# Weight conversion in an attention and two-layer kernel: the shift on ScalarE, the scaling inside VectorE's product, two early halves

## The chip, the core and the metric

The kernel runs on one core of a Trainium2 chip. A core has five engines with queues of their own: TensorE (PE; its weight loads are shown as PEld), VectorE (DVE), ScalarE (ACT), GpSimd (POOL) and SyncE (SP), which here issues all DMAs. Each engine takes its instructions in order; semaphores hold an instruction back until its inputs are there. The metric is the device time of one execution in microseconds (us).

## The reference

Block-causal attention over 4 batches of 8 heads, 576 positions of 64 dimensions each, and two feed-forward layers of 2304 tokens, width 512, inner width 2048, everything in float32:

```python
scores = where(block_i >= block_j, q @ k.T / 8, -1e9)          # blocks of 64 positions
attn   = exp(scores - max); attn /= attn.sum() + 1e-9
x      = (attn @ v) as 2304 x 512
h = x @ w_in;  x = (relu(h) ** 2) @ w_out                      # layer 0
h = x @ w_in2; out = (h * cos(h)) @ w_out2                     # layer 1
```

## The kernel before

**Attention.** Two heads form a pair, 16 pairs in all. For a pair, TensorE makes the scores of 9 blocks of rows (line 374; block 8 goes to the tile `wide`), VectorE takes their maxima (386), ScalarE the exponentials with their sums (391), GpSimd and VectorE the inverse of the sums (416, 422), GpSimd scales the rows `P` (431). TensorE transposes `P` in groups of four blocks (452); ScalarE rounds each group to `PTh` (457), VectorE keeps the rest as `PTl` (460), which also frees the PSUM bank. TensorE multiplies with the values (517), and ScalarE, VectorE and GpSimd put the two heads' results into `xall` (528, 531, 534, 537). GpSimd also scales the keys (357) and splits the values (486, 492).

The order of these steps on every engine is made by `Plan`: each step has an engine, a cost and a rank; the planner keeps a clock for each engine and takes, among the steps that can start earliest, that of the smallest rank. `RANK` holds an offset for each kind of step, to which ten times the pair's number is added. The order that comes out is the order of the program.

**Weights.** A product in float32 is made of three products of rounded halves (high x high, high x low, low x high), so each weight must be split. The weights come as a packed pair of words of 64 bits, `raw`, with a low and a high word. There are 64 pieces ("halves", class `Half`): 2 layers x 16 channels x 2 (`w0` for the hidden product, `w1` for the output product). Converting one half is: shift (line 205, low word right by 9), mask (212) and rebias (218, ScalarE) of the high word's bits, join (223, puts the lower bits of the high word over the low word), fraction (229, ScalarE, the low word as a float scaled by 2^-43), sign (235), power (241, the exponent alone), high (256, ScalarE, or 259 on GpSimd: the rounded high part) and low (265, fraction times power: the rest). Unless an engine is named, VectorE does it.

The first `EARLY` = 4 halves are steps of the attention plan (`add_half`); the key `late` holds them back until the last pair's first scores, and their rank is 1000. Two more are only loaded there. All others are converted by `convert()`, called while the layers run: one call ends an old half and begins a new one, with four `raw` buffers and two `bits` buffers; fraction is put off to the next call of `flush()`.

**Layers.** Each layer goes over blocks of up to 512 tokens (five in each layer), each block over 16 channels `c`. A step (`hidden`, line 629) makes 12 matmuls into one of four banks `h`; ScalarE and VectorE make `g` of it and split it into `gs` (651, 652, 641, 644 in layer 0; 659, 662, 667, 673, 676 in layer 1); three steps later `output` (line 693) uses it in 12 matmuls. `PACE` says how many conversions are called in a step of each block; the first block converts layer 0, the last block of layer 0 and those behind it convert layer 1, each half when its buffer is free. Before each block but the first, `xall` is split into `xs` (315 on ScalarE, 318 on VectorE), into the same buffers as before.

## Time and profile before

| | |
|---|---|
| median of 3 runs | 1008.35 us (1008.33 to 1009.51) |
| profiled execution, its own time | 1007.74 us |
| its span in the trace | 1006.0 us |
| TensorE busy | 980.9 us (98%) |
| VectorE, ScalarE, GpSimd busy | 624.1, 594.2, 168.4 us |
| mean granted clock of TensorE | 0.996 |

The page of a profile lists the busy time of each engine and the costliest lines. Matmuls are pipelined, and their ends are modelled, so a busy TensorE is not one at its peak. What a change is worth is read from the stage that it touches: attention ends at about 192 us; block 0 of layer 0, with the conversion of its weights, goes to about 289 us; the weights of layer 1 are converted between 500 and 750 us.

### The profile page before, as it was taken

What the parts mean: (1) busy time and instruction counts of PE and PEld (TensorE: products, weight loads), DVE (VectorE), ACT (ScalarE), POOL (GpSimd) and SP (SyncE); (2) the same over time, 40 slices, a digit from 0 to 9 for tenths busy, and PEclk for the clock granted to TensorE, in tenths of its full rate; (3) what the DMA queues carried; (4) which work ended last, traced back from release to release, by engine and by line L of the source; (5) the groups of instructions that cost most, each with busy time, mean ns of one, the idle gap of its engine ahead of it and who ended that gap; (6) DMA issues with size and microseconds to landing.
All of it is one profiled execution on the core that took longest, in us unless ns stands there. A gap on an engine that the chain in (4) does not pass through costs nothing.

```text
span 1006.0 us, 13923 instructions
## 1 busy us (share of the span) xinstructions
PE 980.9 (98%) x4895; PEld 824.7 (82%) x4895; DVE 624.1 (62%) x1260; ACT 594.2 (59%) x1226; POOL 168.4 (17%) x290
## 2 busy tenths in 40 slices
PE   9999999889989999999999999999999999999998
PEld 7878887767768889988888888888888888899996
DVE  6888789899951111221168998976646555656554
ACT  7999999688873344443367886644334333434433
POOL 6888888700000000000000000000000000000000
PEclk9999999999999999999999999999999999999999
DMA  6433321244420000000013432000000100100000
GB/s 219 143 107 123 112 97 63 85 167 168 168 84 1 1 1 1 2 1 1 1 63 115 170 135 84 22 1 35 8 1 1 43 1 1 43 1 1 33 1 31
DMA packets 18806, 58.56 MB, mean 58 GB/s; under 512 B 1968, under 2 KB 2096, under 8 KB 18736
## 3 DMA queue, kind: packets, MB, share of 16 engines
q1 hardware_dynamic: 18736, 57.68, 16.5%
q8 instruction: 38, 0.62, 0.2%
q14 instruction: 32, 0.26, 0.1%
HBM read 52.95 MB, written 4.72 MB: 57 GB/s over the span
## 4 chain that ended last, share of the span: by engine, by line
PE 72%; DVE 19%; ACT 5%; issue 3%; POOL 1%; DMA 0%; SPq 0%; DVEq 0%; ACTq 0%
PE acc L693 32%; PE h L629 31%; PE ps L374 3%; DVE w L265 3%; DVE bits L235 3%; DVE raw L223 3%; PE ps L452 2%; PE ps L517 2%; DVE raw L205 2%; DVE raw L241 2%; DVE nmax L386 2%; DVE gs L644 2%; ACT P L391 1%; ACT PTh L457 1%; DVE PTl L460 1%
## 5 line engine op out<-in xcount | busy, mean ns | idle before, releaser
L629 PE MATMUL h<-xs,w 128*128 128x512 f32 (+2 forms) x1920 | 421.7, 368 | 3.5 <-ACT xs L315 3.0
L629 PEld LDWEIGHTS h<-xs,w 128*128 128x128 f32 x1920 | 344.6, 188 | 60.2 <-ACT xs L315 3.4
L693 PE MATMUL acc<-gs,w 128*128 128x512 f32 (+1 forms) x960 | 215.2, 372 | 9.0 <-DVE gs L644 8.9
L693 PE MATMUL acc<-w,gs 128*128 128x512 f32 x864 | 209.8, 391 | 0.3 <-ACT xall L706 0.3
L693 PEld LDWEIGHTS acc<-gs,w 128*128 128x128 f32 x960 | 168.4, 190 | 43.8 <-DVE gs L644 13.5
L644 DVE TENSOR_TENSOR gs<-g,gs 128x512 fp32r<-128x512 f32 (+2 forms) x160 | 101.1, 633 | 143.6 <-ACT gs L641 143.5
L693 PEld LDWEIGHTS acc<-w,gs 128*128 128x128 f32 x864 | 161.6, 188 | 33.0 <-ACT xall L706 0.8
L641 ACT CAST gs<-g 128x512 fp32r<-128x512 f32 (+2 forms) x160 | 92.3, 577 | 152.6 <-DVE g L676 96.0
L662 DVE SCALAR_TENSOR_TENSOR g<-turns,h 128x512 f32<-128x512 int32 (+1 forms) x80 | 50.7, 634 | 122.2 <-ACT turns L659 121.6
L659 ACT ACTIVATE turns<-h 128x512 int32<-128x512 f32 (+1 forms) x80 | 44.2, 552 | 68.1 <-PE h L629 68.0
L651 ACT ACTIVATE g<-h 128x512 f32<-128x512 f32 (+1 forms) x80 | 43.9, 549 | 67.5 <-PE h L629 66.8
L374 PE MATMUL ps<-kB,qB 128*128 128x64 f32 (+7 forms) x256 | 81.7, 416 | 1.5 <-DVE PTl L460 0.8
L431 POOL TENSOR_SCALAR P<-P,rinv 128x64 f32<-128x64 f32 (+2 forms) x144 | 79.8, 573 | 6.6 <-DVE rinv L422 3.1
L673 ACT ACTIVATE g<-g,half_pi 128x512 f32<-128x512 f32 (+1 forms) x80 | 54.6, 682 | 38.1 <-DVE g L667 38.1
L452 PEld LDWEIGHTS ps<-ident,P 128*128 128x128 f32 (+1 forms) x400 | 49.1, 142 | 27.7 <-issue 14.8
L460 DVE TENSOR_TENSOR PTl<-ps,PTh 128x512 fp32r<-128x512 f32 x96 | 65.2, 686 | 6.9 <-ACT PTh L457 5.4
L391 ACT ACTIVATE P<-ps,nmax 128x64 f32<-128x64 f32 (+7 forms) x128 | 65.4, 513 | 6.4 <-DVE nmax L386 4.9
L452 PE MATMUL ps<-ident,P 128*128 128x128 f32 (+1 forms) x400 | 63.4, 280 | 3.5 <-POOL P L431 3.1
L386 DVE TENSOR_REDUCE nmax<-ps 128x1 f32<-128x64 f32 (+7 forms) x128 | 56.4, 444 | 10.2 <-PE ps L374 9.2
L457 ACT CAST PTh<-ps 128x512 fp32r<-128x512 f32 (+1 forms) x112 | 60.1, 551 | 4.3 <-PE ps L452 3.4
L517 PE MATMUL ps<-PTh,vhl 128*128 128x320 f32 (+3 forms) x224 | 59.5, 299 | 1.2 <-DVE PTl L460 0.7
L218 ACT ACTIVATE bits<-bits,new_bias 128x512 int32<-128x512 int32 x64 | 46.5, 726 | 17.6 <-DVE bits L212 17.6
(52 smaller groups left out, 959.8 us busy)
## 6 DMA issues: line engine op xcount, KB each, us to landing
raw<-in_w_dram SPq DMA_DIRECT2D x64, 512.0 KB, 3.6
qB<-in_qd_dram SPq DMA_DIRECT2D x15, 576.0 KB, 4.0
v_raw<-in_vp_dram SPq DMA_DIRECT2D x16, 320.0 KB, 2.9
kB<-in_kT_dram SPq DMA_DIRECT2D x16, 288.0 KB, 2.8
out_dram<-o SPq DMA_DIRECT2D x8, 512.0 KB, 3.1
out_dram<-o SPq DMA_DIRECT2D x2, 256.0 KB, 2.9
qB<-in_qd_dram SPq DMA_DIRECT2D x1, 384.0 KB, 4.4
qB<-in_qd_dram SPq DMA_DIRECT2D x1, 192.0 KB, 2.9
```

Of the source, the lines that this page charges most:

```text
L374: nc.tensor.matmul(bank[:, 0:w] if one else wide[:, x, 0:w], lhsT=qB[r][:, i].rearrange("p e d -> p (e d)"), rhs=kB[r][:, x * w : (x + 1) ...
L386: nc.vector.tensor_reduce(out=nmax[i], in_=held(), axis=AX.X if one else AX.XY, op=ALU.max, negate=True)
L391: nc.scalar.activation(out=mine if one else mine.rearrange("p (x w) -> p x w", x=2), in_=held(), func=AF.Exp, bias=nmax[i], scale=1.0, acc ...
L431: nc.gpsimd.tensor_scalar(out=mine, in0=mine, scalar1=inverse[:, i - i0 : i - i0 + 1], scalar2=1.0, op0=ALU.mult, op1=ALU.mult,)
L452: nc.tensor.transpose(bank[0:keys, n * 128 : (n + 1) * 128], P[r][:, o : o + keys], ident)
L457: nc.scalar.copy(out=PT[0][0:keys, at], in_=plan.held[s][0][0:keys, 0:w])
L460: nc.vector.tensor_tensor(out=PT[1][:, at] if keys == 128 else PT[0][keys:128, at], in0=bank[0:keys, 0:w], in1=PT[0][0:keys, at].bitcast(F32),
L517: nc.tensor.matmul(bank[:, (a - i0) * D : w], lhsT=vhl[:, j, e].rearrange("p x d -> p (x d)"), rhs=pt[x][:, s0 : s0 + i1 - a, e, :], start ...
L629: nc.tensor.matmul(h, lhsT=w[:, a, kk * 128 : (kk + 1) * 128], rhs=xs[kk].parts[:, x], start=(m == 0), stop=(m == 3 * KD - 1),)
L641: nc.scalar.copy(out=gs[:, 0], in_=g)
L644: nc.vector.tensor_tensor(out=gs[:, 1], in0=g, in1=gs[:, 0].bitcast(F32), op=ALU.subtract)
L693: nc.tensor.matmul(dst, lhsT=lhsT, rhs=rhs, start=(c == 0 and m == 0), stop=(c == KF - 1 and m == 2),)
```

## The change

Shift goes from VectorE to ScalarE, as a multiplication by a little under 2^-9 from integer to integer. Fraction is no longer an instruction of its own: its factor 2^-43 is put into low, which becomes a product of two operations on VectorE (integer low word x 2^-43 x power). `flush`, `later`, `fraction` and `high_beside` fall away; in `convert()` the order is now sign, shift, mask, high, power, rebias, low, join. `EARLY` is 2 instead of 4, and the two early halves round their high part on ScalarE. In the plan they have no `late` any more; a new argument `beside` lets a step hold a second engine's clock, and each of VectorE's five steps of an early half is planned as holding GpSimd as well. All ranks change; the early halves' goes from 1000 to 206.6. `PACE` of the last block of layer 0 goes from 1.75 to 2.

```diff
-    "scores": 3.5,
-    "maximum": -3.1,
+    "scores": 5.2,
+    "maximum": -5.2,
...
-    "weights": 1000,
+    "weights": 206.6,
...
+            if beside:
+                t = max(t, clock[beside])
+                clock[beside] = t + cost
...
-    EARLY = 4
+    EARLY = 2
...
         def shift(self):
-            nc.vector.tensor_scalar(
-                out=self.low_word, in0=self.low_word, scalar1=9, scalar2=None,
-                op0=ALU.logical_shift_right,
+            nc.scalar.activation(
+                out=self.low_word.bitcast(U32), in_=self.low_word.bitcast(U32), func=AF.Copy,
+                scale=2.0**-9 * (1.0 - 2.0**-23),
             )
...
-        def fraction(self):
-            nc.scalar.activation(
-                out=self.low_word.bitcast(F32), in_=self.low_word.bitcast(U32), func=AF.Copy,
-                scale=2.0**-43,
-            )
...
         def low(self):
-            nc.vector.tensor_tensor(
-                out=self.room()[:, 1], in0=self.low_word.bitcast(F32),
-                in1=self.high_word.bitcast(F32), op=ALU.mult,
-            )
+            nc.vector.scalar_tensor_tensor(
+                out=self.room()[:, 1], in0=self.low_word.bitcast(U32), scalar=2.0**-43,
+                in1=self.high_word.bitcast(F32), op0=ALU.mult, op1=ALU.mult,
+            )
...
             new.shift()
+            new.mask()
         if old:
+            old.high()
             old.power()
-            old.high()
         if new:
-            new.mask()
             new.rebias()
         if old:
             old.low()
         if new:
             new.join()
-            later.append(new.fraction)
...
-                plan.add("V", 0.34, rank, x.shift, [late], [raw])
-                plan.add("V", 0.34, rank, x.mask, [high, late], [bits])
...
+                both = dict(beside="G")
+                plan.add("A", 0.56, rank, x.shift, writes=[raw])
+                plan.add("V", 0.45, rank, x.mask, [high], [bits], **both)
...
-        PACE = {0: 2, last: 1.75, last + 1: 0.75}
+        PACE = {0: 2, last: 2, last + 1: 0.75}
```

Lines of the changed kernel have other numbers: 216 is mask, 227 join, 233 sign, 239 power, 257 low, 209 shift; 444 is `PTl` (460 before), 436 the transposes (452), 358 the scores (374), 515 the join into `xall` (531), 627 `gs` low (644).

The first place is VectorE in block 0 of layer 0, one conversion between two `gs` low. Before:

```order
L644 TENSOR_TENSOR gs<-g,gs 128x512
L235 SCALAR_TENSOR_TENSOR bits<-raw,bits 128x512
L205 TENSOR_SCALAR raw<-raw 128x512
L241 TENSOR_SCALAR raw<-bits 128x512
L212 TENSOR_SCALAR bits<-raw 128x512
L265 TENSOR_TENSOR w_2320<-raw 128x512
L223 SCALAR_TENSOR_TENSOR raw<-raw 128x512
```

And now:

```order
L627 TENSOR_TENSOR gs<-g,gs 128x512
L233 SCALAR_TENSOR_TENSOR bits<-raw,bits 128x512
L216 TENSOR_SCALAR bits<-raw 128x512
L239 TENSOR_SCALAR raw<-bits 128x512
L257 SCALAR_TENSOR_TENSOR w_2331<-raw 128x512
L227 SCALAR_TENSOR_TENSOR raw<-raw 128x512
```

The shift is gone, and mask, which stood between power and low, now stands ahead of power.

The second place is TensorE where pair 2's transposes (of `P_98`) stand among pair 3's scores (`ps<-kB,qB`). Before:

```order
L452 MATMUL ps_85<-ident,P_98 128x128 x4
L374 MATMUL ps_87<-kB_94,qB_92 128x256
L452 MATMUL ps_84<-ident,P_98 128x128 x4
L374 MATMUL ps_83<-kB_94,qB_92 128x320
L452 MATMUL ps_86<-ident,P_98 128x128 x4
L374 MATMUL ps_88<-kB_94,qB_92 128x384
L452 MATMUL ps_85<-ident,P_98 128x128 x4
L374 MATMUL ps_87<-kB_94,qB_92 128x448
L452 MATMUL ps_84<-ident,P_98 128x128 x4
L374 MATMUL ps_83<-kB_94,qB_92 128x512
```

And now:

```order
L436 MATMUL ps_84<-ident,P_98 128x128 x4
L358 MATMUL ps_87<-kB_94,qB_92 128x192
L358 MATMUL ps_86<-kB_94,qB_92 128x256
L358 MATMUL ps_85<-kB_94,qB_92 128x320
L358 MATMUL ps_83<-kB_94,qB_92 128x384
L358 MATMUL ps_87<-kB_94,qB_92 128x448
L358 MATMUL ps_88<-kB_94,qB_92 128x512
L436 MATMUL ps_84<-ident,P_98 128x128 x4
L436 MATMUL ps_86<-ident,P_98 128x128 x4
L436 MATMUL ps_85<-ident,P_98 128x128 x4
L436 MATMUL ps_83<-ident,P_98 128x128 x4
```

The scores stand together and the transposes behind them; two pairs on the same happens once more, and from there on the two kinds alternate again.

The third place is VectorE at the last pair, whose transposes are lowered there to `PTl`. Before:

```order
L235 SCALAR_TENSOR_TENSOR bits<-raw,bits 128x512
L205 TENSOR_SCALAR raw<-raw 128x512
L241 TENSOR_SCALAR raw<-bits 128x512
L531 TENSOR_TENSOR xall<-ps_85,half_117 64x320
L265 TENSOR_TENSOR w_2104<-raw 128x512
L212 TENSOR_SCALAR bits<-raw 128x512
L223 SCALAR_TENSOR_TENSOR raw<-raw 128x512
L460 TENSOR_TENSOR PTl<-ps_84,PTh 128x512
L460 TENSOR_TENSOR PTl<-ps_86,PTh 128x512
```

And now:

```order
L406 RECIPROCAL rinv_116<-sums_113 128x2
L444 TENSOR_TENSOR PTl<-ps_83,PTh 128x512
L515 TENSOR_TENSOR xall<-ps_85,half_117 64x320
L444 TENSOR_TENSOR PTl<-ps_84,PTh 128x512
L444 TENSOR_TENSOR PTl<-ps_86,PTh 128x512
```

The conversion's instructions are no longer there; those of the two early halves now stand among pairs 1 to 4 (counted from 0).

## Rows read from the trace of the kernel before

**Rows 1.** Busy us and counts of each engine in four stretches, whole core.
```profile
core 0: us, PE busy (x) PEld busy (x) DVE busy (x) ACT busy (x) POOL busy (x), PEclk, DMA share, GB/s
20.00:50.00 30.00, 29.81 (x193) 25.04 (x194) 24.10 (x58) 28.51 (x85) 26.17 (x43) 1.00 0.48 164
...
180.00:192.00 12.00, 8.86 (x57) 8.16 (x56) 9.71 (x20) 8.42 (x18) 10.28 (x11) 0.86 0.24 88
...
220.00:280.00 60.00, 55.65 (x235) 43.11 (x234) 60.00 (x126) 51.07 (x89) 0.00 (x0) 1.00 0.48 167
300.00:350.00 50.00, 50.00 (x223) 41.40 (x222) 7.52 (x11) 17.74 (x29) 0.00 (x0) 1.00 0.00 1
```

**Rows 2.** Waits of TensorE, 190 to 320 us: us, times, longest.
```profile
PE acc L693 <- DVE gs L644: 8.9, 11, 4.1
```

**Rows 3.** Waits of TensorE, 320 us to the end, its only row.
```profile
PE acc L693 <- ACT xall L706: 0.3, 1, 0.3
```

**Rows 4.** Waits of TensorE, 0 to 205 us.
```profile
PE ps L452 <- POOL P L431: 3.1, 3, 1.1
...
PE ps L374 <- DVE PTl L460: 0.8, 1, 0.8
PE ps L517 <- DVE PTl L460: 0.7, 1, 0.7
```

**Rows 5.** Timeline of TensorE: start, us, what [idle before, releaser].
```profile
185.82 3.04 PE L452 MATMUL ps<-ident,P 128*128 128x128 f32 x13 [1.07 <-POOL P L431]
...
192.06 9.18 PE L629 MATMUL h<-xs,w 128*128 128x512 f32 x38
...
289.25 0.50 PE L629 MATMUL h<-xs,w 128*128 128x512 f32 x1 [2.99 <-ACT xs L315]
```

**Rows 6.** Timeline of VectorE in block 0, one step.
```profile
276.46 0.68 DVE L644 TENSOR_TENSOR gs<-g,gs 128x512 fp32r<-128x512 f32 x1
277.06 0.68 DVE L235 SCALAR_TENSOR_TENSOR bits<-raw,bits 128x512 int32<-128x512 int32 x1
277.67 0.42 DVE L205 TENSOR_SCALAR raw<-raw 128x512 int32<-128x512 int32 x1
278.00 0.42 DVE L241 TENSOR_SCALAR raw<-bits 128x512 int32<-128x512 int32 x1
...
278.68 0.68 DVE L265 TENSOR_TENSOR w<-raw 128x512 fp32r<-128x512 f32 x1
279.28 0.68 DVE L223 SCALAR_TENSOR_TENSOR raw<-raw 128x512 int32<-128x512 int32 x1
...
282.70 0.68 DVE L644 TENSOR_TENSOR gs<-g,gs 128x512 fp32r<-128x512 f32 x1
```

**Rows 7.** Timeline of VectorE in layer 1, two neighbours, the second reading the first.
```profile
606.88 0.69 DVE L662 SCALAR_TENSOR_TENSOR g<-turns,g 128x512 f32<-128x512 int32 x1
607.60 0.43 DVE L667 TENSOR_SCALAR g<-g 128x512 int32<-128x512 int32 x1
```

**Rows 8.** Groups of ScalarE, 207 to 286 us: busy us, mean ns, idle before.
```profile
L218 ACT ACTIVATE bits<-bits,new_bias 128x512 int32<-128x512 int32 x26 | 18.8, 725 | 5.8 <-DVE bits L212 5.8
L229 ACT ACTIVATE raw<-raw 128x512 f32<-128x512 uint32 x25 | 17.0, 678 | 5.5 <-DVE raw L223 5.5
```

**Rows 9.** Timeline of VectorE, the fourth early half's low.
```profile
196.03 0.91 DVE L265 TENSOR_TENSOR w<-raw 128x512 fp32r<-128x512 f32 x1
```

**Rows 10.** Timeline of ScalarE: relu of hidden 1 and of hidden 14, `xs`.
```profile
207.54 0.58 ACT L651 ACTIVATE g<-h 128x512 f32<-128x512 f32 x1
...
286.80 0.57 ACT L651 ACTIVATE g<-h 128x512 f32<-128x512 f32 x1
...
288.58 2.18 ACT L315 CAST xs<-xall 128x512 fp32r<-128x512 f32 x4
```

**Rows 11.** Timeline of GpSimd: an ordinary pair's scaling, the last pair's.
```profile
155.72 3.11 POOL L431 TENSOR_SCALAR P<-P,rinv 128x320 f32<-128x320 f32 x5
...
179.25 4.67 POOL L431 TENSOR_SCALAR P<-P,rinv 128x320 f32<-128x320 f32 x4
```

68 lines of the change are left out of this document (28 added, 40 removed).

## The prediction

> **What bounds the kernel now.** I read the table of stretches first [rows 1]. From 300 to 350 us TensorE is busy for 50.00 of 50 us with VectorE at 7.52: there TensorE sets the pace, and 223 matmuls in 50 us are 5.4 us for the 24 of one step (hidden and output of one channel). From 220 to 280 us it is the other way: VectorE 60.00 of 60, ScalarE 51.07, TensorE 55.65. This is block 0 of layer 0, where every weight is converted as it is first used. The list of waits says the same: TensorE waits 8.9 us for `gs` from VectorE, one wait of 4.1 among them [rows 2]. Later, from 320 us to the end, it waits 0.3 us in all [rows 3], so nothing behind 320 us can be gained. The third loss is the end of attention: the last pair's transposes wait 3.1 us for GpSimd's scaled `P`, and two products wait 0.8 and 0.7 us for `PTl` [rows 4]; TensorE's granted clock is 0.86 of full in 180 to 192 us [rows 1], a mix of its two levels (1.2 and 2.4 GHz) after those waits, and 13 transposes take 3.04 us [rows 5]. Early attention (20 to 50 us) is full: TensorE 29.81 of 30 [rows 1].
>
> So there are three marks. T is the start of the first hidden product, 192.06 in this run. X is the start of block 1's first hidden product, 289.25, after a wait of 2.99 us for `xs` [rows 5]. From X to the end of the span are 1006.0 - 289.25 = 716.75 us, which I keep: they are TensorE's.
>
> **The change part by part.**
>
> *One conversion on VectorE.* One step of block 0 runs from `gs` low at 276.46 to the next at 282.70: 6.24 us, two conversions and one `gs` low [rows 6]. From start to start sign takes 0.61, shift 0.33, power and mask 0.34 each, low 0.60, join 0.60, together 2.82; `gs` low takes 0.60. The change removes the shift (0.33). Low becomes a two-operation form with an integer input; the nearest row, line 662 with an integer and a float input, occupies 0.69 us [rows 7], as low does now (0.68, [rows 6]): nothing to pay. But the new order puts power directly ahead of low, which reads what power writes. Where a dependent instruction stands directly behind its source, it begins only after the source's end: 606.88 + 0.69, next start 607.60, an interval of 0.72 where 0.60 is usual [rows 7]. That gives 0.11 back: power then costs 0.45 instead of 0.34. A conversion is 2.82 - 0.33 + 0.11 = 2.60 and a step 5.8 us; with no such stall it would be 5.6. TensorE's step is 5.4, so VectorE stays the bound, by less.
>
> *One conversion on ScalarE.* Fraction leaves, shift comes: the same Copy over the same integer words. The nearest rows are 0.678 (fraction, line 229) and 0.725 (integer output with a bias, line 218) [rows 8]; I take 0.68, being the same function without a bias. ScalarE's sum a step is unchanged; 51.07 of 60 is busy [rows 1], so it covers this. Dearer, it costs 0.05 x 2 a step, which its idle time covers. Followed through one step (rebias waits for mask, sign for rebias, high for sign) its loop comes out some 0.3 us shorter than VectorE's 5.8.
>
> The Trainium skill ("ScalarE: Activation LUTs", Rules for kernel authors) gives multiplications to VectorE, not ScalarE. The rows bear out the price of one instruction (0.42 as shift on VectorE, 0.68 on ScalarE), but not that it decides here, since VectorE is the full one; by that rule alone the 30 shifts would cost 30 x 0.26 = 8 us.
>
> *Two early halves instead of four, and their place.* Before, two of the four are still being finished when T has come: the fourth ends its low at 196.03 + 0.91 [rows 9], T + 4.9, and GpSimd rounds its high part. Only then does VectorE begin on the layers' own conversions. After, the last pair's rows are followed by the layers' conversions at once. From T: ScalarE needs about 1.0 to empty the last heads' banks (an estimate, two copies), shift starts T + 1.0, rebias is done T + 2.3, the first sign starts there, then 2.60 a conversion with one extra wait of 0.3 for rebias behind the first relu; the relu of hidden 1 comes at T + 9.7. Before, it came at 207.54 [rows 10], T + 15.5. The relu of hidden 14 follows 13 steps later: T + 9.7 + 13 x 5.8 = T + 85.1, before 286.80, T + 94.7 [rows 10]. From there to the first `xs` are 1.78 us (288.58) and 0.67 more to X [rows 5, 10]: X = T + 87.5, before T + 97.2. **Block 0 gives 9.7 us**; bounds 7 (ScalarE's loop at 6.0 a step) and 13 (steps of 5.6 and no wait at the first steps). The two halves that are no longer early cost nothing more: block 0 calls two conversions a step in 16 steps, and before, its last step had only one left. The wait for `xs` stays, since ScalarE's queue still runs behind TensorE.
>
> *End of attention.* VectorE no longer converts between the last pairs' steps. GpSimd's four last tiles took 4.67 us beside that, where five such tiles take 3.11 in an ordinary pair [rows 11]; less the largest (about 0.7) that is 2.4, so 2.3 come back, and the two waits on `PTl` (1.5). **4 us**; at least 0.8 (the last pair has nothing to overlap, and only the `PTl` waits go), at most 3.1 + 1.5 and 1.3 for slow transposes, 5.9.
>
> *The early halves' new place.* They are now done in pairs 1 to 4, behind nothing but attention's own steps. Each adds 5 VectorE instructions (2.9 us), 3 on ScalarE (2.0, at some 0.68) and, for GpSimd, the slowing just named. In 20 to 50 us VectorE has 5.9 idle, GpSimd 3.8, ScalarE only 1.5 [rows 1], and 4.0 are added to ScalarE. Also the table of ranks groups TensorE's work there: six scores in a row, then six groups of transposes, twice, where before they alternate. VectorE frees a transpose group's bank at 0.6 us apiece, slower than TensorE fills them, and the first of the six waits for a bank that VectorE frees only behind five maxima: about 1 us at each place. **I charge 2 us**, between 0 (the idle time swallows it) and 4 (2 at each place).
>
> That DVE work slows GpSimd is what the Trainium skill says in "SBUF — State Buffer" (Who interferes with whom): the pair of ports that both share is locked for a whole instruction. The trace agrees, with the 4.67 us against 2.4. By the lock alone the two halves hold GpSimd for up to 2 x 2.9 = 5.8 us, 2.0 above its idle time: the same charge.
>
> *Second refill* (500 to 640 us). The rate in the last block of layer 0 goes from 1.75 to 2 conversions a step: 1.75 x 2.82 + 0.60 = 5.5 becomes 5.8, against TensorE's 5.4. Over 11 such steps VectorE falls 0.4 x 11 = 4.4 us behind; before, its 9 full steps fell 0.8 x 9 behind less two steps of 2.0 gained, about 3. TensorE then waited 0.3 us at most [rows 3], so 1.4 more should still be covered by the output products that stand between. Zero; up to 2.5 if the cover is gone. Loads keep their place: four raw buffers, each requested when low has read it and used three conversions later (7.8 us).
>
> *Sum.* -9.7 - 4.0 + 2.0 = -11.7. T becomes 190.1, X 277.6, the span 994.3. The profiled execution took 1007.74, 1.74 above its span, and the median of the runs is 1008.35, 0.6 above that: 996.7 on the median's scale. I say **996.5**.
>
> **The rivals.**
> *A: TensorE sets the pace of block 0 too.* If the dependent neighbour costs nothing and attention's end loses all 5.9, steps are 5.6 and little is charged early: 13 + 5.9 - 0.5 = 18, 990. For it: VectorE's plain sum. Against it: two measured intervals of 0.72 and the wait for `xs`.
> *B: ScalarE takes VectorE's place.* Shift, high and rebias now stand in one chain with sign and relu. If semaphores add 0.3 a step, the step is 6.1: block 0 gives 5.8, attention's end 2, the early places cost 3: gain 5, 1003. For it: ScalarE's 51 of 60 [rows 1]. Against it: its sum is unchanged.
> *C: slower: the new ranks open a wait in every pair of attention.* All ranks change, not only those of the weights. TensorE has nearly no idle time there now (0.19 in 30 us, [rows 1]), so each wait is lost. From 13.7/15 = 0.9 us a pair on, the gain of 13.7 (9.7 and 4.0) is eaten; at 1.3 a pair the time is 1008.35 - 13.7 + 19.5 = 1014. For it: ScalarE's 28.51 of 30. Against it: behind pair 4 the order of TensorE alternates scores and transposes as before.
> *D: the change doesn't do what it says*: low's two-operation form takes the shift's 0.33 back. Then a step is 6.4; the relu of hidden 14 comes at T + 10.7 + 13 x 6.4 = T + 93.9, block 0 gives 0.8, and in all 2.8 are left: 1005.5. Line 662's 0.69 speaks against it.
>
> **How the numbers follow.** Forecast (992 to 1000) 0.57, A 0.14, B 0.14, D 0.05, C 0.06, and 0.04 for sums that cancel within 2 us. The runs of one kernel tell 0.2% apart, 2 us. Faster 0.90, same 0.04, slower 0.06. The range reaches over A and most of B and leaves out the rest, about 2 in 10: 989.5 to 1003.5.
>
> **What would show it.** A step of block 0, from `gs` low to `gs` low, is 5.8 us (5.6 is A, 6.1 B, 6.4 D), with power to low 0.45 apart. TensorE's waits in block 0 name `w` from VectorE rather than `gs`. Shift on ScalarE takes 0.68. X minus T is 87.5. T is 190: later than 192 means the new place or the new ranks cost more than the end of attention returns, and the waits of TensorE between 20 and 50 us say which. A wait of over 1 us near 600 us would mean that the second refill is no longer covered.

## The result, and the profile after

The changed kernel takes 1000.3 us (median of 4 runs, 998.36 to 1001.27) against 1008.93 us of the kernel before in the same comparison: a ratio of 0.9911, interval 0.9894 to 0.9929. That is 8.6 us less; the forecast was 996.5, by a sum of 11.7 less. The profiled execution took 1001.27 us, the slowest of the four, with a span of 999.4 us against 1006.0, so the traces below differ by 6.6 us. The other 2 us of the gain lie between these two executions and the medians, and no trace places them.

Four marks divide the span. W is the first product into `wide`, the 576-wide scores, of pair 0 (9.45 us before, 9.69 after; the start-up in front of it differs by some tenths from one execution to another). The last pair's wide is the same product of the last pair. T is the first hidden product, X the first hidden product of block 1, as in the prediction.

```
                        before   after   difference   forecast
W                         9.45    9.69      +0.24        -
W to last pair's wide   155.83  159.73      +3.90       +2.0
last pair's wide to T    26.78   21.15      -5.63       -4.0
T to X                   97.19   88.31      -8.88       -9.7
X to end of span        716.75  720.52      +3.77        0
```

The sum is -6.6. The first three terms went the way the prediction says, each with its size somewhat off; the last was not foreseen at all. The lines that answer to [rows 1], busy time by stretch, with three stretches more:

```profile
core 0: us, PE busy (x) PEld busy (x) DVE busy (x) ACT busy (x) POOL busy (x), PEclk, DMA share, GB/s
20.00:50.00 30.00, 28.14 (x181) 23.48 (x182) 26.91 (x61) 28.63 (x81) 24.97 (x41) 1.00 0.49 164
180.00:192.00 12.00, 10.79 (x77) 9.63 (x76) 7.06 (x16) 9.06 (x22) 8.04 (x13) 1.00 0.00 1
...
220.00:280.00 60.00, 57.08 (x235) 42.59 (x234) 58.23 (x112) 54.56 (x95) 0.00 (x0) 0.99 0.55 183
270.00:290.00 20.00, 17.19 (x61) 12.95 (x60) 14.72 (x27) 15.04 (x27) 0.00 (x0) 0.83 0.37 120
550.00:600.00 50.00, 49.39 (x217) 40.33 (x216) 47.04 (x90) 43.84 (x76) 0.00 (x0) 1.00 0.50 167
```

In 20 to 50 us TensorE lost 1.7 us of busy time and 12 products. At the end of attention (180 to 192) it gained 1.9 us and runs at a clock of 1.00 instead of 0.86. In block 0 VectorE is still all but full. In 270 to 290 the clock is 0.83 where it was 1.00 before, and in 550 to 600, where the second refill runs, 217 matmuls stand for 223.

TensorE's waits from 190 to 320 us, after, answer to [rows 2] (us in total, times, longest; the last two lines are of its weight loads):

```profile
PE h L612 <- ACT xs L299: 2.8, 1, 2.8
PE h L612 <- ACT w L254: 1.2, 1, 1.2
PEld h L612 <- DVE w L257: 5.9, 13, 0.6
PEld h L612 <- ACT w L254: 4.1, 13, 1.6
```

The 8.9 us for `gs` are gone. TensorE is now held back at its weight loads: 13 times by the low part of `w` from VectorE and 13 times by the high part from ScalarE, which itself waits for VectorE's sign (shown further down). A hidden group takes 3.10 us from start to start (270.11 to 273.21) instead of 2.72. The transition to block 1 in TensorE's timeline (start, us, what, idle before):

```profile
270.11 3.26 PE L612 MATMUL h<-xs,w 128*128 128x512 f32 x12
273.21 2.88 PE L676 MATMUL acc<-gs,w 128*128 128x512 f32 x12
278.88 5.79 PE L612 MATMUL h<-xs,w 128*128 128x512 f32 x12 [2.79 <-ACT xs L299]
284.46 3.33 PE L676 MATMUL acc<-gs,w 128*128 128x512 f32 x12
287.63 2.88 PE L612 MATMUL h<-xs,w 128*128 128x512 f32 x12
```

X comes after a wait of 2.79 us (before 2.99, [rows 5]). But the 12 products behind it take 5.58 us from start to the next start; before they took 3.39 (289.25 to 292.64, with 0.23 of waiting for the next `xs` in it). That, and 0.45 in the next group (3.17 instead of 2.72), is the fall of the clock: 2.6 us in this execution, which the prediction did not have.

One step of VectorE in block 0, which answers to [rows 6]:

```profile
271.28 0.69 DVE L627 TENSOR_TENSOR gs<-g,gs 128x512 fp32r<-128x512 f32 x1
271.88 0.68 DVE L233 SCALAR_TENSOR_TENSOR bits<-raw,bits 128x512 int32<-128x512 int32 x1
272.48 0.42 DVE L216 TENSOR_SCALAR bits<-raw 128x512 int32<-128x512 int32 x1
272.82 0.42 DVE L239 TENSOR_SCALAR raw<-bits 128x512 int32<-128x512 int32 x1
273.34 0.69 DVE L257 SCALAR_TENSOR_TENSOR w<-raw 128x512 fp32r<-128x512 uint32 x1
...
277.16 0.68 DVE L627 TENSOR_TENSOR gs<-g,gs 128x512 fp32r<-128x512 f32 x1
```

From `gs` to `gs` 5.88 here, 5.81 in most steps of block 0. The shift is gone, low takes 0.69, and power holds the queue for 0.45 to 0.52 before low starts.

### The profile page after: what moved, and what is told of

It is laid out like the page before. It is cut to its first block, busy times and chain, and to the rows that moved or that the text cites. A ratio compares the mean times of both kernels' runs of the same rounds, so it can differ in the third digit from the quotient of the medians.

```text
span 999.4 us, 13751 instructions
## 1 busy us (share of the span) xinstructions
PE 983.4 (98%) x4895; PEld 823.0 (82%) x4895; DVE 607.7 (61%) x1196; ACT 593.5 (59%) x1230; POOL 161.0 (16%) x286
## 4 chain that ended last, share of the span: by engine, by line
PE 77%; DVE 16%; ACT 4%; POOL 1%; issue 1%; DMA 0%; SPq 0%; DVEq 0%; ACTq 0%
PE acc L676 32%; PE h L612 31%; PE ps L358 5%; PE ps L501 5%; PE ps L436 3%; DVE w L257 3%; DVE bits L233 3%; DVE raw L227 3%; DVE raw L239 2%; DVE bits L216 2%; DVE gs L627 1%; PE wide L358 1%; ACT P L375 1%; POOL P L415 1%; DVE nmax L370 1%
## 5 line engine op out<-in xcount | busy, mean ns | idle before, releaser
L612 PE MATMUL h<-xs,w 128*128 128x512 f32 (+2 forms) x1920 | 428.9, 371 | 4.9 <-ACT xs L299 3.2
L676 PE MATMUL acc<-gs,w 128*128 128x512 f32 (+1 forms) x960 | 210.6, 368 | 0.0
L254 ACT CAST w<-bits 128x512 fp32r<-128x512 f32 x64 | 39.5, 618 | 20.1 <-DVE bits L233 15.7
```

The source lines that it names most:

```text
L612: nc.tensor.matmul(h, lhsT=w[:, a, kk * 128 : (kk + 1) * 128], rhs=xs[kk].parts[:, x], start=(m == 0), stop=(m == 3 * KD - 1),)
L676: nc.tensor.matmul(dst, lhsT=lhsT, rhs=rhs, start=(c == 0 and m == 0), stop=(c == KF - 1 and m == 2),)
```

## The experiments

All times are measured beside the kernel before, and each ratio goes against the runs of before in the same comparison (medians 1008.9 to 1009.8 us). The marks come from each kernel's trace; W to wide is the part among the pairs, wide to T the tail. Each row of marks is one execution. The diffs are excerpts; `...` stands for lines left out.

```
kernel                      W to wide  wide to T  T to X  X to end  median    ratio
before                       155.83     26.78     97.19   716.75   1008.93   1
after                        159.73     21.15     88.31   720.52   1000.30   0.9911
conversion only              155.60     26.24     89.90   718.18   1001.09   0.9923
order only                   161.71     22.34     93.05   719.37   1007.11   0.9982
after, xs first              159.73     21.16     86.50   716.86    995.78   0.9870
after, join first            159.75     21.16     85.37   717.67    995.63   0.9866
after, rate 1.75             159.69     21.16     88.34   717.63    998.34   0.9891
after, early at end          158.17     26.34     88.30   719.27   1004.03   0.9947
after, no early              158.16     25.08     89.60   719.49   1003.15   0.9935
three edits                  159.70     21.15     83.61   716.06    992.13   0.9825
three, old ranks             161.84     22.40     83.84   716.02    994.05   0.9852
three, three early           164.01     21.17     83.67   717.57    997.65   0.9883
after, GpSimd not held       160.57     21.18     88.29   719.23   1001.61   0.9923
three, early in mid pairs    163.44     22.35     82.43   716.05    996.10   0.9863
```

Four theories were to be tested: that VectorE's chain sets block 0's step and the conversion alone shortens it (theory 1); that the slow products at X come from a clock that falls after the wait (theory 2); that the second refill at two halves a step costs over a microsecond (theory 3); that the early halves are what the pairs lose (theory 4 and what came of it).

**The conversion alone.** The kernel before, with the three calls changed and `convert()` in the new order:

```diff
         def shift(self):
-            nc.vector.tensor_scalar(
-                out=self.low_word, in0=self.low_word, scalar1=9, scalar2=None,
...
+            nc.scalar.activation(
+                out=self.low_word.bitcast(U32), in_=self.low_word.bitcast(U32), func=AF.Copy,
+                scale=2.0**-9 * (1.0 - 2.0**-23),
...
-        def fraction(self):
...
         def low(self):
-            nc.vector.tensor_tensor(
...
+            nc.vector.scalar_tensor_tensor(
+                out=self.room()[:, 1], in0=self.low_word.bitcast(U32), scalar=2.0**-43,
...
```

> The kernel before with the new conversion alone (shift on ScalarE, scaling inside VectorE's low, the order sign, shift, mask, high, power, rebias, low, join); four early halves, the old ranks, the old place and a rate of 1.75 halves a step in the second refill are kept. Theory 1 (VectorE's chain sets the step of block 0, and the conversion alone shortens it from 6.24 to 5.8 us): gs low follows gs low after 5.8 us in block 0, the first hidden product starts near 192 as before, and block 1's starts at about 192 + 97.2 - 16 x 0.44 = 282, against 289.25; the time is about 1009 - 7 = 1002, a ratio of 0.993, or 0.995 if the clock falls after the wait for xs as it does in the changed kernel. Rival (the order of attention and the two early halves carry the gain, and low takes back what shift and stall leave): step 6.2, block 1 near 289, ratio 0.999 or more.

Measured: 0.9923 (0.991 to 0.9935). VectorE's `gs` low in this kernel:

```profile
229.71 0.69 DVE L630 TENSOR_TENSOR gs<-g,gs 128x512 fp32r<-128x512 f32 x1
235.53 0.68 DVE L630 TENSOR_TENSOR gs<-g,gs 128x512 fp32r<-128x512 f32 x1
```

A step of 5.82, and X at 281.52 where 282 was expected. Theory 1 holds. X to the end is 1.4 us longer than before; the first hidden product of block 1 takes 4.90 us there (281.52 to 286.42), the slow clock again.

**The order alone.** The changed kernel with shift, fraction and low as before, and the rate of the second refill at 1.75:

```diff
...
-    plan.add("A", 0.56, rank, x.shift, writes=[raw])
+    plan.add("V", 0.45, rank, x.shift, writes=[raw], **both)
...
+    plan.add("A", 0.52, rank, x.fraction, writes=[raw])
...
-        PACE = {0: 2, last: 2, last + 1: 0.75}
+        PACE = {0: 2, last: 1.75, last + 1: 0.75}
...
```

> The changed kernel with the old conversion (shift on VectorE, the fraction on ScalarE, the product in low, the old order of the calls); two early halves planned as holding GpSimd and the new ranks are kept, the rate of the second refill is set back to 1.75. Theory 1: the last pair's 512-wide scores at about 178 (before 175), the first hidden product at about 190.6, then about 10.5 us to the first relu and 13.5 steps of 6.24 us, so block 1 at about 285 (before 289.25, changed kernel 278.88); the time is about 1009 - 4 = 1005, a ratio of 0.996. Rival (block 0 runs faster for want of the two halves, not for the conversion): block 1 near 280 and a ratio of 0.992.

Measured: 0.9982 (0.9973 to 0.999), a gain of 1.8 us and not 4. The step is 6.23 us, as theory 1 says; the rival's X near 280 did not come (286.73). T to X is 93.05, 4.1 less than before, with no early half left over behind T. What the expectation missed is T, 193.68 instead of 190.6: with the old conversion's early steps, one VectorE instruction more for each half, the last pair's wide scores come 161.71 us after W. The two parts alone, -7.8 and -1.8 us by their ratios, add to -9.6; together, at the same rate of 1.75, they give -11.0 ("after, rate 1.75"). The 1.4 us between these sums are within the intervals. The traces show a difference all the same: with the old conversion the same two early halves end 2.0 us later among the pairs (161.71 against 159.69) and the tail takes 1.2 us more (22.34 against 21.16). So the shorter conversion also makes the early halves easier to place.

**xs ahead of the last step's other work.** In the loop over steps the next block's `xs` copies are called before relu, square and `gs` instead of behind them:

```diff
+            if step < len(steps) and c == KF - 1 and i + 1 < len(blocks):
+                xs = [Cut(*blocks[i + 1][1:], kk) for kk in range(KD)]
+                for x in xs:
+                    x.high()
+                    x.low()
             for a, z in zip_longest(begin, [None] + end):
...
-            if step < len(steps) and c == KF - 1 and i + 1 < len(blocks):
-                xs = [Cut(*blocks[i + 1][1:], kk) for kk in range(KD)]
-                for x in xs:
-                    x.high()
-                    x.low()
```

> The changed kernel with the xs copies and differences of the next block called ahead of the relu, square and gs of the step in which they are called, instead of behind them; nothing else. Theory 2 (TensorE's clock falls to 0.83 in 270 to 290 because of the 2.79 us wait for xs just before it): ScalarE's xs comes about 1.8 us earlier (relu, square and gs high, 0.61 + 0.66 + 0.52, no longer stand ahead of it), block 1 starts at about 276.5 to 277, the wait is about 0.7 to 1 us, the first hidden products take about 3.4 instead of 5.58 us at a clock of 0.95 or more, and the time falls by 1.8 + 2.6 = 4.4 us against the changed kernel, to about 996. Rival (the fall of the clock has nothing to do with the wait): only the 1.8 us, about 998.5. Rival (the delayed gs is waited for instead): a wait acc<-gs appears within the next three steps, and the time stays at 1000.

Measured: 0.987 (0.9854 to 0.9885), 995.78 us where 996 was expected. TensorE at the transition, and the stretch 270 to 290:

```profile
277.34 0.50 PE L612 MATMUL h<-xs,w 128*128 128x512 f32 x1 [0.98 <-ACT xs L299]
278.16 2.81 PE L612 MATMUL h<-xs,w 128*128 128x512 f32 x11 [0.32 <-DVE xs L302]
280.81 2.88 PE L676 MATMUL acc<-gs,w 128*128 128x512 f32 x12
```

```profile
270.00:290.00 20.00, 18.69 (x80) 14.47 (x79) 14.90 (x27) 17.07 (x30) 0.00 (x0) 1.00 0.36 124
```

T to X is 1.81 shorter, the first group takes 3.47 us at a clock of 1.00, and no new wait for `gs` appears. The slow clock went with the wait: the mean clocks of the four runs are 0.999 to 1.000, those of the changed kernel 0.996 to 0.999. Of the 3.66 us that X to end gives back, 2.56 are the two groups named above (5.58 to 3.47 and 3.17 to 2.72). The other 1.10 lie at the end of the second refill, where the wait for `xs` near 590 us went as well.

**Join between power and low.**

```diff
-        if old:
-            old.low()
         if new:
             new.join()
+        if old:
+            old.low()
```

> The changed kernel with the new half's join called ahead of the old half's low, so that low no longer stands right behind power, whose result it reads. Theory 1 (VectorE's chain sets the step): power to the next instruction takes 0.34 instead of 0.45 us, twice a step, so the step of block 0 is 5.8 - 0.23 = 5.57 us and block 1 starts about 14 x 0.23 = 3.2 us earlier, at 275.7; the time is about 997. Rival (ScalarE's shift, which join reads, or the weights that come 0.6 us later in the chain, hold the step at 5.8): no difference, 1000.3.

Measured: 0.9866 (0.9852 to 0.988), 995.63 us. VectorE's step:

```profile
230.82 0.42 DVE L239 TENSOR_SCALAR raw<-bits 128x512 int32<-128x512 int32 x1
231.19 0.69 DVE L227 SCALAR_TENSOR_TENSOR raw<-raw 128x512 int32<-128x512 int32 x1
231.80 0.69 DVE L257 SCALAR_TENSOR_TENSOR w<-raw 128x512 fp32r<-128x512 uint32 x1
```

Power now takes 0.33 to 0.37 and the step 5.60 us (229.28 to 234.88). T to X is 2.94 us shorter; 3.2 was expected. The gain is larger than that because X to end gains 2.85 more: 1.80 behind block 1's second hidden product (222 matmuls in 550 to 600 us, and no wait of TensorE past 330 us, at the same rate of two halves a step), and 1.05 ahead of it, where the clock still falls behind a wait of 2.00 us, but less (4.79 us for the first group; as the last section shows, this differs from one execution to another). So the stall in VectorE's queue was costing in both places, and the dearer rate is covered once the step is 5.6.

**The rate of the second refill.**

```diff
-        PACE = {0: 2, last: 2, last + 1: 0.75}
+        PACE = {0: 2, last: 1.75, last + 1: 0.75}
```

> The changed kernel with the rate of the second refill (block 4, the last of layer 0) set back from 2 to 1.75 halves a step; nothing else. Theory 3 (with 2 halves VectorE's step is 5.88 us there, over TensorE's 5.44, and by the block's end the wait for xs costs 0.6 us and the slower feed the six matmuls that 550 to 600 lacks): 222 to 223 matmuls in 550 to 600, no wait for xs at 590, and 0.6 to 1.4 us less, 999 to 999.7. Rival (the refill's end runs into layer 1 if it is slower, since two halves fewer are converted by each eighth step): the waits stand in 600 to 650 instead, and the time is 1000.3 or up to 1 us more.

Measured: 0.9891 (0.9877 to 0.9904), 998.34 us: 2 us by the ratios, more than expected. The stretch:

```profile
550.00:600.00 50.00, 50.00 (x223) 41.38 (x222) 45.46 (x86) 42.67 (x72) 0.00 (x0) 1.00 0.44 147
```

From block 1's second hidden product to the end are 709.96 us (286.74 to 996.7), in the changed kernel 711.77 (287.63 to 999.4): 1.8 us are the refill. No wait was moved into layer 1; TensorE waits for nothing past 330 us. In the changed kernel all of the 1.8 stands at two places, read from start to start of the groups of 12 products (elsewhere in this part of the run a full-width group takes 2.72 us). The first is the start of the next block:

```profile
590.08 0.50 PE L612 MATMUL h<-xs,w 128*128 128x512 f32 x1 [0.38 <-ACT xs L299]
590.80 2.79 PE L612 MATMUL h<-xs,w 128*128 128x512 f32 x11 [0.22 <-DVE xs L302]
```

The output group ahead of it, from 586.81, and the hidden group itself, up to 593.43, take 3.27 and 3.35 us, 1.18 too much (the six matmuls fewer in 550 to 600 us: 6 x 0.22 = 1.3); the waits in brackets name only 0.60 of it. The second is at 607.03, where a copy that empties the banks is waited for: 3.07 and 3.01, 0.64 too much, with 0.18 named. The kernel before loses 0.66 there too (at 613.58) and nothing at the start of the block, so the dearer rate itself costs 1.2.

**The early halves back at the end.**

```diff
-    "weights": 206.6,
+    "weights": 1000,
...
+                late = f"S{NPAIR - 1}.0"
...
+                plan.add("A", 0.56, rank, x.shift, [late], [raw])
+                plan.add("V", 0.45, rank, x.mask, [high, late], [bits], **both)
```

> The changed kernel with the two early halves kept back: their rank is 1000 again and their shift and mask wait for the last pair's first scores, as before the change; all other ranks are the new ones. Theory 4 (the 3.9 us between pairs 1 and 4 are the price of the two halves there): the last pair's 576-wide scores start near 165.5 (169.42 in the changed kernel, 165.28 before), its 512-wide ones at 174.2; the two halves then cost 0 to 4 us in the tail, whose 12.45 us become 12.5 to 16.5; the first hidden product at 187 to 191, and the time 997 to 1000.7. Rival (the new ranks of the attention's own steps cost it): the wide scores of the last pair stay near 169, and the tail's price comes on top, 1001 to 1004.

Measured: 0.9947 (0.9935 to 0.9959), 3.6 us slower than the changed kernel. The wide scores of the last pair came at 167.89, between the two theories: without halves among them the pairs still take 2.3 us longer than before. So of the 3.9 us about 1.6 are the halves and 2.3 the new ranks, as totals. The tail took 26.34 us, nearly as long as before, with a clock of 0.86 in 182 to 194 us, and the waits of TensorE in it are the old ones:

```profile
PE ps L436 <- POOL P L415: 3.1, 4, 1.7
PE ps L436 <- DVE PTl L444: 0.5, 1, 0.5
```

Two halves cost 5.2 us in the tail (26.34 less 21.15) and 1.6 among the pairs. Their new place is worth 3.6, and that is what the time says.

**No early halves.** `EARLY = 0`; nothing else.

> The changed kernel with no early halves at all (four halves are still loaded ahead); the first hidden product then waits for two conversions after the attention. It measures what the two halves cost among the pairs and what they save behind. Theory 4: wide scores of the last pair near 165.5, the attention's last product 4 us earlier, near 186.5; then some 6 us until the first hidden product, and block 0 with two more halves of 2.56 us of VectorE each (5.8 - 0.69 over 2); block 1 at 278.9 - 4 + 5.1 = 280 or up to 3 us later, the time 1001 to 1004. Rival (ranks): wide scores near 169 and the time 1005 to 1008.

Measured: 0.9935 (0.9922 to 0.9948), 1003.15 us, inside what theory 4 gave, but by another sum. The wide scores came at 167.63 and not at 165.5, which confirms the 2.3 us of the ranks. The start of the layers:

```profile
188.74 0.22 PE L501 MATMUL ps<-PTh,vhl 128*128 128x64 f32 x1
192.71 13.52 PE L612 MATMUL h<-xs,w 128*128 128x512 f32 x45 [3.75 <-ACT w L254]
```

The wait is 3.75 us and not 6. Block 0 then takes 89.60 us instead of 88.31: the two halves more do not cost 5.1 us in it but 1.3. The prediction's sentence that halves which are no longer early cost block 0 next to nothing, since it makes two conversions in each of its 16 steps anyway, is borne out.

**Three edits at once:** xs first, join first, rate 1.75.

> The changed kernel with three edits at once: xs ahead of relu, square and gs; join ahead of low; 1.75 halves a step in the second refill. If the parts add, as theories 1 and 2 say: block 1 at 275.93 (join first) less 1.5 (xs first) = 274.4, the clock at 1.00 through 270 to 290, the first hidden product 3.4 us, and the time 995.6 - 1.5 - 1.4 = 992.7, 0.9835 of before. Rival (the two gains are the same one, the wait for xs and the clock behind it, taken once): 995 to 995.7.

Measured: 992.13 us (991.87 to 992.33), 0.9825 (0.9813 to 0.9838): this is the fastest kernel here. The parts add if what they share is counted once: T to X gives the 1.81 us of the first edit and the 2.94 of the second (4.70 in all), and X to the end, where each edit had taken some of the same losses, gives the 2.6 of the clock and the 1.8 of the refill (4.46).

```profile
274.34 0.51 PE L612 MATMUL h<-xs,w 128*128 128x512 f32 x1 [0.25 <-ACT xs L299]
275.07 2.79 PE L612 MATMUL h<-xs,w 128*128 128x512 f32 x11 [0.22 <-DVE xs L302]
277.70 2.88 PE L676 MATMUL acc<-gs,w 128*128 128x512 f32 x12
```

The wait is 0.25, the first group takes 3.36 us, and X to end is 716.06.

**The old ranks, with the early halves in their new place.** On the kernel with the three edits, all offsets of the attention's own steps as before; the halves stay at 206.6.

```diff
-    "scores": 5.2,
-    "maximum": -5.2,
...
+    "scores": 3.5,
+    "maximum": -3.1,
...
     "weights": 206.6,
```

> The kernel with the three edits (xs first, join first, 1.75 halves a step) with all ranks of the attention's own steps as before the change; the two early halves stay at their new rank, 206.6, planned as holding GpSimd. Theory 5 (without any early half the pairs still end 2.35 us later than before the change, 167.63 against 165.28, so the new ranks cost that much among the pairs): the last pair's wide scores at 167.2 instead of 169.58, the tail as long as with the new ranks (12.5 us), the first hidden product at 188.3 instead of 190.73, the time 989.8. Rival (what the new ranks lose among the pairs they give back in the tail): the tail takes 14 to 16 us, and the time is 991 to 994.

Measured: 0.9852 (0.9837 to 0.9866), 994.05 us, 2.7 us (by the ratios) slower than with the new ranks. Theory 5 falls. The pairs take 161.84 us, longer still than with the new ranks (159.70): with these halves among them the old ranks lose 6 in this trace. A part of that is the clock of this execution, the slowest of the five (996.04 us): it fell behind a wait of 1.86 us that ended at 44.09 (clock 0.57 in this stretch).

```profile
44.00:48.00 4.00, 3.91 (x15) 2.85 (x15) 2.36 (x6) 2.04 (x6) 2.79 (x7) 0.57 0.51 145
```

The two runs with a mean clock of 1.000 took 993.58 and 993.79 us. Less those 2.3 us the halves cost some 4 with the old ranks (an estimate), as much as halves and new ranks together (3.9). The tail takes 22.40, 1.25 more. So the 2.3 us are not a price of the new ranks that could be had back with these halves in place.

**Three early halves.** `EARLY = 3` on the kernel with the three edits.

> The kernel with the three edits, with three early halves instead of two, at the same rank and planned as holding GpSimd. Theory 6 (a half among the pairs costs 0.9 us, half of the 169.42 - 167.63 = 1.8 that two cost, and a half in block 0 (5.60 - 0.69) / 2 = 2.46 us of VectorE's chain): the first hidden product 0.9 us later, block 1 1.5 us earlier, the time 990.6. Rival (the third half costs more than the first two, since it collides with GpSimd's work of one more pair): the first hidden product over 2.5 us later and the time 992 or more.

Measured: 0.9883 (0.9869 to 0.9897), 997.65 us. Theory 6 falls on both counts. The third half cost 4.3 us among the pairs (164.01 against 159.70), more than the two others together. And it saved nothing: T to X is 83.67 against 83.61. The waits for the third half's weights (1.2 and 0.5 us in the kernel with the three edits) are gone, but the first `gs` low comes 10.74 us after T in both kernels (205.60 and 201.47) and the steps last 5.60 in both: each step makes two conversions whatever lay ready. The time saved early on is waited at X, 2.2 us for `xs`, and the clock falls once more (4.90 us for the first group).

**GpSimd not held in the plan.** The changed kernel without `beside`:

```diff
-    plan.add("V", 0.45, rank, x.mask, [high], [bits], **both)
+    plan.add("V", 0.45, rank, x.mask, [high], [bits])
...
-    plan.add("V", 0.75, rank, x.low, [raw, high], **both)
+    plan.add("V", 0.75, rank, x.low, [raw, high])
```

> The changed kernel with the two early halves planned for VectorE alone, not as holding GpSimd; same ranks and costs. Theory 7 (VectorE's early instructions collide with GpSimd's, as the power of 1.78 us at 40.49 shows, and the plan's holding keeps most of them apart): more of the early instructions take over 1 us, the last pair's wide scores come at 170.4 to 172.4 instead of 169.42, the time is 1001 to 1003. Rival (holding GpSimd idle in the plan costs as much as the collisions would): wide scores at 168.5 to 169.5 and the time 999.5 to 1000.5.

Measured: 0.9923 (0.9909 to 0.9936). The intervals of this and of the changed kernel overlap; the trace says 0.84 us among the pairs (160.57 against 159.73) and nothing from there to X. The direction is theory 7's, at a smaller size and not clear of noise, but not its mechanism: no early VectorE instruction takes over 0.82 us here, and TensorE's loss shows under another name, GpSimd's scaled `P`, for which it waited nowhere in 20 to 180 us in the changed kernel:

```profile
PE ps L436 <- POOL P L415: 2.3, 5, 1.1
```

**The early halves in pairs 6 and 9,** on the kernel with the three edits:

```diff
+                late = f"S{6 + 3 * n}.0"
...
+                plan.add("A", 0.56, rank, x.shift, [late], [raw])
+                plan.add("V", 0.45, rank, x.mask, [high, late], [bits], **both)
```

> The kernel with the three edits (xs first, join first, 1.75 halves a step) with the two early halves held back until the first scores of pair 6 and of pair 9, instead of starting in pair 1 and following each other; they stay at rank 206.6, planned as holding GpSimd. Theory 8 (the price of a half depends on what it meets: among pairs 1 to 4 loads, the first cuts of xs and the halves crowd together, and an early instruction stretches to 1.78 us; among the steady pairs of 11.03 us VectorE has 2 us free in each): without halves the last pair's wide scores come at 167.63, the two cost 0 to 1 us there, so at 167.6 to 168.7 instead of 169.58, the first hidden product at 188.8 to 189.9 instead of 190.73, the time 990.3 to 991.4. Rival (the halves cost the same wherever they stand, since ScalarE and GpSimd are nearly full in the steady pairs): wide scores at 169.2 or later, the time 991.8 to 993.

Measured: 0.9863 (0.9843 to 0.9884), 996.1 us, slower by 3.8. Theory 8 falls, and so does its rival, which was too mild: the two cost 5.3 us there (163.44 less 158.16), over three times as much as in pairs 1 to 4. VectorE (first two lines) and GpSimd (third) at one place:

```profile
75.52 1.95 DVE L227 SCALAR_TENSOR_TENSOR raw<-raw 128x512 int32<-128x512 int32 x1
77.40 0.68 DVE L444 TENSOR_TENSOR PTl<-ps,PTh 128x512 fp32r<-128x512 f32 x1
```

```profile
75.39 1.54 POOL L476 TENSOR_TENSOR vhl<-v_raw,vhl 128x640 fp32r<-128x640 f32 x1
```

VectorE's join, started 0.13 us behind GpSimd's product, ends 0.54 us after that has ended (76.93): it ran its own usual time only then. The same at 110.72, 1.65 us for a sign beside the same GpSimd step. Behind it stands `PTl`; TensorE's waits from 20 to 180 us name ScalarE's `P` (2.1 us) and `PTl` (0.7). How much of the 5.3 us the stretched instructions cause is not shown.

## Why the prediction was right, and where it was not

The measured 1000.3 lies inside the stated range, and 0.3 us outside the narrower 992 to 1000 to which the forecast gave 0.57. The three terms that were forecast make -10.6 in the traces, against -11.7; what takes the time off the forecast is the fourth, X to the end.

*Block 0, -9.7 forecast, -8.9 measured.* The mechanism stands at every step. VectorE's step is 5.81 us (5.8 forecast), low's new form takes 0.69 (rival D's 6.4 is out), and power in front of low takes 0.45, the dependent neighbour of [rows 7]; when join was put between, 0.11 came back twice a step and the step was 5.60. ScalarE's shift takes 0.68 us, and ScalarE does not set the pace (rival B's 6.1 is out), in its groups of 207 to 286 us:

```profile
L222 ACT ACTIVATE bits<-bits,new_bias 128x512 int32<-128x512 int32 x25 | 18.1, 723 | 0.0
L209 ACT ACTIVATE raw<-raw 128x512 uint32<-128x512 uint32 x25 | 17.0, 682 | 0.0
L254 ACT CAST w<-bits 128x512 fp32r<-128x512 f32 x25 | 15.4, 617 | 6.9 <-DVE bits L233 6.9
```

All its waiting is for VectorE's sign. The 0.8 us that are missing: the relu of hidden 1 came at 200.64, T + 10.1 instead of T + 9.7, and 13 steps took 75.8 us instead of 75.4 (relu of hidden 14 at 276.42). From there to X were 2.46 us, 2.45 forecast.

*End of attention, -4.0 forecast, -5.6 measured,* near the bound of 5.9. The row that answers to the transposes of [rows 5]:

```profile
185.50 1.64 PE L436 MATMUL ps<-ident,P 128*128 128x128 f32 x13 [0.65 <-POOL P L415]
```

The 13 transposes take 1.64 us at full clock (3.04 before), the waits for GpSimd's `P` 1.2 instead of 3.1 us in all, and those for `PTl` [rows 4] are gone. GpSimd is as fast in the last pair as in any other, as the prediction says: 0.62 us a tile on average, where it was 1.17 before [rows 11].

```profile
182.17 1.86 POOL L415 TENSOR_SCALAR P<-P,rinv 128x384 f32<-128x384 f32 x3
```

The waits give 1.9 and 1.5 us, the clock at the 13 transposes 1.4, together 4.8 of the 5.6; the rest is not assigned. The step that was undersized is above all the clock: it was left in the upper bound and not put into the term. That the work of VectorE's halves was the cause is shown by putting two of them back: the tail is 26.34 us again.

*The early halves' new place, +2.0 forecast, +3.9 measured,* just under the bound of 4. The reason given was only half of it. The places are right, by the starts of the wide scores: after the change they fall back by 1.2 us between 31.60 and 44.35 (12.75, before 11.54), by 2.0 between 56.07 and 69.70 (13.63, before 11.64), and by 0.7 in all elsewhere. The prediction's mechanism there was VectorE's rate of freeing banks behind six groups of transposes. What the trace shows is GpSimd and VectorE in each other's way. VectorE first, then GpSimd, then TensorE's waits of that pair:

```profile
40.49 1.78 DVE L239 TENSOR_SCALAR raw<-bits 128x512 int32<-128x512 int32 x1
42.20 2.47 DVE L444 TENSOR_TENSOR PTl<-ps,PTh 128x512 fp32r<-128x512 f32 x4
```

```profile
40.44 1.55 POOL L476 TENSOR_TENSOR vhl<-v_raw,vhl 128x640 fp32r<-128x640 f32 x1
```

```profile
PE ps L436 <- DVE PTl L444: 1.1, 1, 1.1
```

An early power, which usually takes 0.42 us, starts 0.05 us behind GpSimd's `vhl` and ends 0.28 after it. Behind it stand four `PTl`, and TensorE waits 1.1 us for the first bank: most of that pair's loss. The plan holds GpSimd for the early instructions just to keep this apart, but it goes by its own clock, and on the chip the two met by 50 ns. The Trainium skill says in "SBUF — State Buffer" (Who interferes with whom) that the two share a pair of ports, and that for a VectorE instruction that needs it (two inputs in SBUF, or a two-port mode) whoever issues first has it for the whole instruction while the other stands still. The trace agrees: 1.78 us here, 1.95 and 1.65 in pairs 6 and 9, each ending 0.3 to 0.6 us behind GpSimd's end. The prediction had used the same rule the other way round only, VectorE slowing GpSimd. In 56.07 to 69.70 no early instruction is stretched; TensorE waits 0.6 us for a copy of ScalarE and 0.3 for `PTl`, and what makes up the rest of the 2.0 is not settled. Nor can the 1.6 and 2.3 us of the experiments be laid to these places: without early halves the pairs lose nothing up to 64.82 us (10.85 and 11.16 in the two before it), and then 13.11 and 12.47 go by up to 90.41, where 11.42 and 11.00 did before. Halves and ranks change the order together, and only the totals can be split.

That rival C did not come true is shown by the same rows: from 81.17 on, a pair takes 11.02 to 11.03 us, before 10.98 to 11.06. The sum of the prediction's two terms in attention, -2.0, is near the measured -1.7, but that is luck: one error took back the other.

*X to the end, kept at 716.75, measured 720.5.* Here two steps failed. First, the second refill was put at zero ("up to 2.5 if the cover is gone"): VectorE was to fall 1.4 us further behind, and that was to stay covered. The next block's `xs`, before and after:

```profile
594.54 2.18 ACT L315 CAST xs<-xall 128x512 fp32r<-128x512 f32 x4
```

```profile
589.41 2.18 ACT L299 CAST xs<-xall 128x512 fp32r<-128x512 f32 x4
```

Before, the copies begin together with the output group that stands ahead of the next block's first hidden product (both at 594.54); that group takes 2.72 us and the product follows the start of the copies by 0.67 at the least (589.41 to 590.08), so 2.05 us were to spare. After, they begin 2.60 us behind the start of that group (586.81): the lag against TensorE grew by 2.60, not 1.4, and used up the 2.05. The product comes 0.55 us late, and its own group takes 0.63 more, 1.2 in all. From block 1's second hidden product to the end the kernel before takes 710.64 us, the changed kernel 711.77, and the kernels at rate 1.75 or with join first 709.96 to 709.98. (So 0.7 us could be gained behind 320 us, where the prediction reads from [rows 3] that nothing can.) The sign that it names, a wait of over 1 us near 600, did not show: the list has 0.38 and 0.22, and the loss is read from start to start. Second, X to the end was called TensorE's and kept, without a look at its clock behind the wait for `xs`. In the traced execution before, the clock stayed at 1.00 from 285 to 300 us behind 2.99 us of waiting [rows 5]; in the traced execution after, it fell behind 2.79. This is 2.6 us. In the four traced kernels in which that wait is 0.20 to 0.98 us it did not fall, and the time followed.

Where VectorE sets the pace, a fall cost nothing. The kernel before has one in block 0, behind its longest wait for `gs` (clock 0.66 in 209 to 214 us):

```profile
208.67 4.38 PE L693 MATMUL acc<-gs,w 128*128 128x512 f32 x11 [4.11 <-DVE gs L644]
```

There `gs` still follows `gs` after 6.23 us (207.94 to 214.17), VectorE's step.

*What is left open.* When the clock falls. The length of the wait alone does not tell: in the traces it held after 2.99 us in the kernel before and fell after 1.70 in the kernel with the conversion alone. Each trace is one execution, and the executions of one kernel differ. Of the changed kernel's four runs one shows a mean clock of 0.999 and took 998.36 us, so there the fall at X, if any, was small. The traced execution of the kernel before has 0.996; of 44 other runs of it 33 have 0.991 to 0.993, so more of their time was at the low level, and where is not known. That the clock held at X in the one that was traced may be chance, and so may be a part of the 2.6 us. TensorE had waited 0.49 us in each step of block 0 before (55.65 busy of 60, [rows 1]) and was fuller after; whether that matters was not tried.

## What to carry to other kernels

When a stage is bound by one engine's queue, count not only durations but neighbours: an instruction that reads what the one ahead of it wrote costs 0.1 us more here, and an independent one put between them was worth 4.7 us by the medians, over half of what the change gave. A wait that is kept is not free of consequences: look at the granted clock behind it, in the new kernel as in the old, and in more than one execution. Work that is moved into the idle time of a full pipeline is to be priced by what stands behind it in the queue, here the copies that free TensorE's banks, and not by the sum of idle time; the same two halves cost 1.6, 5.2 or 5.3 us, by where they stood. Where the list of waits looks clean, compare the time from start to start: it showed twice what the list named at 590 us.

## What the runs showed of the chip

- After a wait of 1.70 to 3.86 us at X the first 12 products took 4.5 to 5.6 us in nine kernels, with a granted clock of 0.83 to 0.91 in 270 to 290 us (a mix of its two levels, 1.2 and 2.4 GHz); after waits of 0.20 to 0.98 us they took 3.35 to 3.47 us in four kernels. The one traced execution of the kernel before, with 2.99 us and 3.39, is the exception.
- What the fall costs varies with the execution: behind the same wait of 2.79 us the group took 5.58, 4.95, 4.78 and 4.64 us in four kernels that are alike up to there but for the early halves. The spread of the runs goes with it: the changed kernel's four runs took 1001.27, 1000.51, 1000.08 and 998.36 us at mean clocks of 0.996, 0.998, 0.998 and 0.999; the kernel that hardly waits at X took 991.87 to 992.33.
- An early VectorE instruction that starts just behind GpSimd's `vhl` (1.55 us) waits for its end: 1.78, 1.95, 1.65 and, with the old ranks, 1.21 us instead of 0.42 to 0.69. A reciprocal of VectorE that starts 0.37 us behind the same GpSimd step shows no such stretch (0.17 us at 110.64, with the halves in pairs 6 and 9).
